# Attention's small products moved to stand in front of p_packed @ w_in, with four PSUM banks as one ring

## The chip, the core and the metric

The kernel runs on one core of a Trainium2 chip. The core has a matrix engine (TensorE; PE is its matmul row and PEld its weight loads in the profile), a vector engine (DVE), a scalar engine (ACT), GpSimd (POOL) and a queue that issues transfers (SP). Matmul results land in PSUM, which holds 8 banks of 512 float32 columns on 128 partitions. The metric is the device time of one execution in microseconds (us), as the median of several runs.

## The reference, cut to what matters

```python
def sm_attn(qq, kk, vv):
    s = scale * np.matmul(qq, kk.transpose(0, 1, 3, 2))
    s = s - np.max(s, axis=-1, keepdims=True)
    a = np.exp(s)
    a = a / (np.sum(a, axis=-1, keepdims=True) + 1e-09)
    return np.matmul(a, vv)
p_packed = sm_attn(p, k, v)               # p: 8 x 8 x 32 x 64; k, v: 8 x 8 x 576 x 64
out = sm_attn(q, p_packed, p_packed)      # q: 8 x 8 x 576 x 64
x = out with the heads side by side       # 4608 x 512
h = x @ w_in                              # w_in: 512 x 2048
g = np.maximum(h, 0.0) + np.log1p(np.exp(-np.abs(h)))
return g @ w_out                          # w_out: 2048 x 512
```

Everything is float32.

## The kernel before, in words

There are 8 batches of 576 tokens. The second attention of a batch is `a2 @ p_packed`, so x @ w_in is computed as `a2 @ (p_packed @ w_in)`. The small product `p_packed @ w_in` comes from `make_m` (line 690, PSUM tiles `psm`), in chunks of 512 of the 2048 hidden columns; two PSUM tiles (one for each group of four heads, which the text calls a half) make one chunk.

A **unit** is one batch `b` and one block `f` of 128 hidden columns (`f` = 0 to 15). For each unit TensorE runs in this order:

- `gemm1` (line 733): 12 matmuls of 288 columns into two PSUM tiles `ph`;
- four tiles `acc` of the second product (line 772): 3 matmuls of 512 columns each, on the hidden block of two units earlier (`LAG` = 2).

In the second unit (`f` = 1) of an even batch the 64 leftover tokens of two batches are added as 16 more tiles `acc_m`. Their inputs `gh_m` and `gl_m` (lines 745 and 746) are split by DVE into eight pieces, each good for two tiles.

`softplus` turns `ph` into `gh` and `gl`: ACT takes Abs of each half of `ph`, then Exp and Ln; DVE's scalar_tensor_tensor (line 761) reads `ph` for the last time. `weights` and `make_m` also split their results on ACT (a cast) and DVE (a subtraction, `ml`, line 706).

The attention of batch `b + 1` runs as a generator, `attention_next`, in the gaps of batch `b`. Each `next` executes it up to the next `yield`, and each step puts its TensorE work between two `acc` tiles. Its TensorE work for one batch is, in the names used below:

- **s1**: scores of p and k, two PSUM tiles `ps`, line 338, 288 columns, four heads side by side in 64*32 pieces of the array; once alone (first half) and once behind pk (second half);
- **pk**: `packed_products` (line 385), weights of the first softmax times v, 96*32 pieces, six rounds of 64 columns;
- **s2**: scores of q and p_packed, made like s1; once behind pk and once alone;
- **psa** (line 377): three transposes a tile, two tiles a half; **psx** (line 420): one transpose a half.

The order on TensorE is the order of the code. On the other engines a scheduler sets it, by the order of the code and its estimates. Up to the twentieth unit (`PINNED` = 20, batch 1's fourth block) the orders of ACT, DVE, POOL and SP are pinned by tables of numbers. A pace sets how often the generator steps: 0.62 of a step for each `acc` tile in batch 1 and 0.56 from batch 2 on. `make_m` of the chunk that unit `u + 2` starts is called at the end of unit `u`.

PSUM: four banks hold `acc`, two (`ps_h`) hold `ph`, and two (`ps_m`) hold everything that `bank()` hands out: `ps`, `psa`, `psx`, `psm`.

Of the kernel before, what the change touches and what calls it, by code (L numbers as in the profile page):

```python
# [9 lines left out]
F32 = mybir.dt.float32  # L10
# [51 lines left out]
def pack_attention_then_softplus_ffn(  # L62
# [11 lines left out]
    B, H, S, D = q.shape  # L74
    J = p.shape[2]
    DM, DFF = w_in.shape
    P = 128
# [3 lines left out]
    C = S // 2  # L81
# [6 lines left out]
    NF = DFF // P  # L88
    NT = S // P
    REST = S - NT * P  # L90
    LAG = 2
    MC = 512
# [10 lines left out]
    ps_h = ctx.enter_context(tc.tile_pool(name="ps_h", bufs=2, space=bass.MemoryType.PSUM))  # L103
    ps_m = ctx.enter_context(tc.tile_pool(name="ps_m", bufs=2, space=bass.MemoryType.PSUM))
# [17 lines left out]
    PW = BG * J  # L122
    pT = const.tile([P, H, PW], F32, name="pT")

    spare = []

    def bank(nm):
        if spare:
            spare.append(spare.pop(0))
            pool, tag = spare[-1]  # L130
            return pool.tile([P, 512], F32, tag=tag, name=nm)
        return ps_m.tile([P, 512], F32, tag="m", name=nm)
# [285 lines left out]
    def packed_transposed(b, g, pp):  # L418
        ps = bank(f"psx_{b}_{g}")
        nc.tensor.transpose(ps[:, :P], pp.rearrange("x i d -> x (i d)"), ident)  # L420
        pt = small.tile([P, P], F32, tag="pt", name=f"pt_{b}_{g}", bufs=2 * G)
        nc.vector.tensor_copy(pt, ps[:, :P])
        return pt
# [158 lines left out]
    def attention_next(b):  # L582


        a1 = [work.tile([P, S], F32, tag="a1", name=f"a1_{b}_{g}") for g in range(G)]
        if b == FIRST:
            for nm in ("k", "v"):
                for g in range(G):
                    load(nm, b, g)
                    yield  # L590
            yield
        kT = [quads("k", b, 0)]
        yield
        yield
        for c in range(2):
            scores1(b, 0, c, kT[0], a1[0])
        yield
        nm = softmax1_max(b, 0, a1[0])
        kT.append(quads("k", b, 1))
        yield  # L600
        load("q", b, 0)
        z = softmax1_exp(b, 0, a1[0], nm)
        yield
        rs = softmax1_sum(b, 0, z)
        yield
        a1T = work.tile([NP, SI, P], F32, tag="a1T", name=f"a1T_{b}_0", bufs=1)
        for c in range(2):
            a1_transposed(b, 0, c, a1[0], a1T)
            yield
        yield  # L610
        ps = [bank(f"ps1_{b}_{c}") for c in range(2)]
        packed_products(b, 0, a1T, ps[0][:, C:C + D])
        s1 = [products1(b, 1, c, kT[1], ps[c]) for c in range(2)]
        for c in range(2):
            nc.scalar.copy(a1[1][:, c * C:(c + 1) * C], s1[c])
        pp = packed_scaled(b, 0, ps[0][:, C:C + D], rs)
        yield
        load("q", b, 1)
        load("k", b + 1, 0)
        nm = softmax1_max(b, 1, a1[1])  # L620
        qT = [quads("q", b, 0)]
        yield
        z = softmax1_exp(b, 1, a1[1], nm)
        res[b]["pt"].append(packed_transposed(b, 0, pp))
        yield
        rs = softmax1_sum(b, 1, z)
        yield
        a1T = work.tile([NP, SI, P], F32, tag="a1T", name=f"a1T_{b}_1", bufs=1)
        for c in range(2):
            a1_transposed(b, 1, c, a1[1], a1T)  # L630
            yield
        load("k", b + 1, 1)
        qT.append(quads("q", b, 1))
        yield
        ps = [bank(f"ps2_{b}_{c}") for c in range(2)]
        packed_products(b, 1, a1T, ps[0][:, C:C + D])
        s2 = [products2(b, 0, c, qT[0], ps[c]) for c in range(2)]
        pp = packed_scaled(b, 1, ps[0][:, C:C + D], rs)
        a2 = work.tile([P, S], F32, tag="a2", name=f"a2_{b}_0", bufs=2)
        for c in range(2):  # L640
            nc.vector.transpose(a2[:, c * C:(c + 1) * C], s2[c])
        yield
        yield
        load("v", b + 1, 0)
        res[b]["pt"].append(packed_transposed(b, 1, pp))
        yield
        softmax2_exp(b, 0, a2)
        yield
        yield
        softmax2_div(b, 0, a2)  # L650
        yield
        a2 = scores2(b, 1, qT[1])
        yield
        softmax2_exp(b, 1, a2)
        yield
        load("v", b + 1, 1)
        yield
        softmax2_div(b, 1, a2)
        yield

# [50 lines left out]
    def gemm1(b, f, res):  # L711

        n = m_cols(b)
        halves = res["m"][f * P // n]
        at_h, at_l = res["at"]
        phs = [
            ps_h.tile([P, 512], F32, tag="h", name=f"ph_{b}_{f}_{c}")[:, :C] for c in range(2)
        ]
        terms = []
        for g in range(G):  # L720
            mh, ml = halves[g * n // MC]
            o = g * n % MC + f * P % n
            ms = slice(o, o + P)
            xy = [(mh, at_h), (mh, at_l), (ml, at_h)]
            if b and f == 0:
                xy.append(xy.pop(1))
            terms += [(x[:, ms], y, g) for x, y in xy]
        turns = [(i, c) for c in range(2) for i in range(3 * G)]
        if b and f == 0:
            turns.sort(key=lambda x: x[0] == 3 * G - 1)  # L730
        for i, c in turns:
            x, y, g = terms[i]
            nc.tensor.matmul(  # L733
                phs[c], x, y[:, g, c * C:(c + 1) * C], start=(i == 0), stop=(i == 3 * G - 1)
            )
        return phs
# [100 lines left out]
    def pin():  # L837

        traced = list(nc.cur_bb.bb.instructions)
        for engine, order in ORDER.items():  # L840
            kinds = [mybir.InstDMACopy] if engine == mybir.EngineType.SP else COMPUTE
            mine = [i for i in traced if i.engine == engine and type(i) in kinds]
            assert sorted(order) == list(range(len(mine))), (engine, len(order), len(mine))
            for n, i in zip(order[1:], order):
                tc.add_manual_dep(
                    mine[n], mine[i].name,
                    mybir.DependencyInfo(mybir.DependencyClass.NoSync, mybir.DependencyReason.DATA),
                )
            ctx.enter_context(tc.issue_after(mine[order[-1]]))

    PACE = [0.64, 0.62] + [0.56] * B
    FRONT = 1000
    CONV = 1.6
    CONV_EARLY = 1.6
# [39 lines left out]
    for u in range(len(units) + LAG):  # L894
        if u == PINNED:
            pin()
        if u < len(units):
            b, f = units[u]
            if f == 0:
                if (b + 1) % BG == 0 and b + 1 < B:  # L900
                    pack_transposed((b + 1) // BG, pt)
                ahead = attention(b + 1) if b + 1 < B else iter(())
                due = 0.0
            chain = softplus(b, f, gemm1(b, f, res[b]), gs)
            next(chain)
            if f == NF - 1:
                if (b + 2) % BG == 0 and b + 2 < B:
                    pt = load_pack((b + 2) // BG, (nc.sync,))
                for _ in ahead:
                    pass  # L910
                if b + 1 < B:
                    weights(b + 1)
        if u >= LAG:
            b2, f2 = units[u - LAG]
            gh, gl = gs.pop((b2, f2))
            if f2 == 0:
                acc = [ps_acc.tile([P, DM], F32, tag="acc", name=f"acc_{b2}_{t}") for t in range(NT)]
        last = u >= LAG and f2 == NF - 1 and b2 % 2 == 1
        if last:
            both = rests(b2)  # L920
            next(both)
        for t in range(NT):
            if u >= LAG:
                gemm2_tile(
                    acc[t], gh, gl, f2, slice(t * P, (t + 1) * P), f2 == 0, f2 == NF - 1
                )
                if f2 == NF - 1:
                    store(acc[t], [(0, b2, t * P, P)], f"{b2}_{t}", t)
            if u < len(units):
                due += PACE[b] if b else STEPS[f * NT + t]  # L930
                while due >= 1:
                    next(ahead, None)
                    due -= 1
                if b == 0:
                    cdue += CONV
                    while cdue >= 1:
                        next(conv, None)
                        cdue -= 1
            next(chain, None)
        if last:  # L940
            next(both)
        if u + 2 < len(units):


            nb, c = units[u + 2][0], units[u + 2][1] * P
            if c % m_cols(nb) == 0:
                make_m(nb, c // m_cols(nb), res[nb])
# [29 lines left out]
```

## Time and profile before

| | |
|---|---|
| median of 3 runs | 748.07 us (747.09 to 749.26) |
| the profiled execution | 747.87 us, its span 746.0 us |
| PE busy | 715.4 us of the span |
| mean granted TensorE clock | 0.991 of full speed |

The span is what the trace covers; 1.9 us of the profiled execution lie outside it. A timeline row gives the start, the length, the engine, the source line, the operation, the tile written and the tiles read, and the count of instructions merged into it. Matmuls are pipelined: a row's length is longer than its distance to the next row, so the distance between starts is the time that TensorE spends on it.

### The profile page before, as it was taken

The page shows a single profiled execution, that of the slowest core. Times are in us where ns is not written, and L with a number is a line of the kernel's source. Part 1 is how long each engine was busy: PE and PEld are TensorE (multiplying, and loading weights), DVE is VectorE, ACT ScalarE, POOL GpSimd, SP SyncE. Part 2 cuts the span into 40 slices and gives each one's busy share as a digit, 9 for nine tenths or more (in the row PEclk, how much of TensorE's full clock was granted, in tenths as well). Part 3 has the DMA queues.
Part 4 walks back from the last instruction along what each step waited for, and adds up shares of the span by engine and source line. Part 5 has one row for each costly group of instructions (what it writes and reads, how often), then busy time and mean ns, then how long its engine had stood idle before and what let it go on. Part 6 is the DMA issues. An engine that isn't in the chain of part 4 may idle for free.

```text
span 746.0 us, 14398 instructions
## 1 busy us (share of the span) xinstructions
PE 715.4 (96%) x5516; PEld 572.2 (77%) x5516; DVE 515.6 (69%) x1068; ACT 421.0 (56%) x1025; POOL 95.9 (13%) x166
## 2 busy tenths in 40 slices
PE   5479999999999999999999999999999999999997
PEld 3357877777878778777788777877788777888885
DVE  3797779857884587667866678566867568565544
ACT  6679877664553545665553555565553455555540
POOL 1425451100000000000000000100000000101110
PEclk9879999999999999999999999999999999999999
DMA  7846662184113431154104431034403110010002
GB/s 285 308 153 232 170 181 38 46 155 81 40 34 70 65 68 30 49 94 82 33 1 100 67 65 33 0 91 72 88 1 81 32 25 1 0 58 1 1 1 71
DMA packets 143044, 55.97 MB, mean 75 GB/s; under 512 B 116352, under 2 KB 130944, under 8 KB 142976
## 3 DMA queue, kind: packets, MB, share of 16 engines
q1 hardware_dynamic: 142704, 55.00, 29.8%
q8 instruction: 43, 0.70, 0.4%
q14 instruction: 25, 0.20, 0.1%
q10 hardware_dynamic: 272, 0.07, 0.0%
HBM read 45.61 MB, written 9.44 MB: 74 GB/s over the span
## 4 chain that ended last, share of the span: by engine, by line
PE 92%; DVE 3%; DMA 2%; ACT 2%; issue 1%; SPq 0%; DVEq 0%; ACTq 0%
PE acc L772 46%; PE ph L733 28%; PE acc_m L772 6%; PE psm L690 5%; PE ps L338 2%; PE ps L385 1%; PE psa L377 1%; DMA v<-in_v 1%; DMA k<-in_k 1%; ACT e L302 1%; PE psp L412 0%; DVE o L793 0%; DVE t L256 0%; PE psT_k L323 0%; DVE a L440 0%
## 5 line engine op out<-in xcount | busy, mean ns | idle before, releaser
L772 PE MATMUL acc<-wo_h,gh 128*128 128x512 f32 x512 | 206.8, 404 | 0.0
L302 ACT ACTIVATE e<-ph 128x288 f32<-128x288 f32 x256 | 102.6, 404 | 177.5 <-PE ph L733 144.6
L772 PE MATMUL acc<-wo_l,gh 128*128 128x512 f32 x512 | 200.9, 392 | 0.0
L772 PE MATMUL acc<-wo_h,gl 128*128 128x512 f32 x512 | 200.6, 392 | 0.0
L302 ACT ACTIVATE e<-e 128x288 f32<-128x288 f32 (+1 forms) x454 | 188.3, 442 | 6.3
L761 DVE SCALAR_TENSOR_TENSOR e<-ph,e 128x288 f32<-128x288 f32 x230 | 102.7, 453 | 126.2 <-ACT e L302 125.4
L733 PE MATMUL ph<-at_h,mh 128*128 128x288 f32 x512 | 156.3, 306 | 9.4 <-ACT at_h L671 9.2
L733 PE MATMUL ph<-at_l,mh 128*128 128x288 f32 x512 | 150.6, 296 | 1.0 <-DVE at_l L672 1.0
L733 PE MATMUL ph<-at_h,ml 128*128 128x288 f32 x512 | 151.4, 296 | 0.0
L733 PEld LDWEIGHTS ph<-at_h,mh 128*128 128x128 f32 x512 | 96.6, 189 | 42.6 <-DVE gl L746 15.1
L765 POOL COPY rest<-e 128x64 f32<-128x64 f32 x128 | 51.0, 401 | 562.3 <-DVE e L761 531.8
L772 PEld LDWEIGHTS acc<-wo_h,gh 128*128 128x128 f32 x512 | 96.1, 188 | 26.2 <-issue 11.6
L772 PEld LDWEIGHTS acc<-wo_h,gl 128*128 128x128 f32 x512 | 96.1, 188 | 21.1
L772 PEld LDWEIGHTS acc<-wo_l,gh 128*128 128x128 f32 x512 | 96.3, 188 | 13.3
L733 PEld LDWEIGHTS ph<-at_l,mh 128*128 128x128 f32 x512 | 96.3, 189 | 4.6 <-DVE at_l L672 1.3
L733 PEld LDWEIGHTS ph<-at_h,ml 128*128 128x128 f32 x512 | 96.6, 189 | 0.2
L746 DVE TENSOR_TENSOR gl<-e,gh 128x512 fp32r<-128x512 f32 x128 | 87.4, 683 | 6.3 <-PE ph L733 0.5
L705 ACT CAST mh<-psm 128x512 fp32r<-128x512 f32 (+1 forms) x72 | 36.1, 541 | 56.4 <-PE psm L690 56.3
L745 DVE CAST gh<-e 128x512 fp32r<-128x512 f32 x128 | 55.6, 435 | 5.8
L706 DVE TENSOR_TENSOR ml<-psm,mh 128x512 fp32r<-128x512 f32 (+1 forms) x72 | 42.6, 623 | 23.9 <-ACT mh L705 23.9
L690 PE MATMUL psm<-w_in_sb,pt 64*32 64x512 f32 (+1 forms) x576 | 37.3, 553 | 0.4 <-ACT T_q L326 0.2
L265 POOL TENSOR_TENSOR r<-t,r 128x512 int32<-128x512 int32 x16 | 22.9, 1433 | 30.6 <-DVE t L256 22.9
(87 smaller groups left out, 663.5 us busy)
## 6 DMA issues: line engine op xcount, KB each, us to landing
v<-in_v SPq DMA_DIRECT2D x16, 576.0 KB, 5.3
x_i<-in_moe_w_in SPq DMA_DIRECT2D x14, 512.0 KB, 4.6
k<-in_k SPq DMA_DIRECT2D x48, 144.0 KB, 3.1
q<-in_q SPq DMA_DIRECT2D x48, 144.0 KB, 3.1
x_o<-in_moe_w_out SPq DMA_DIRECT2D x11, 512.0 KB, 3.7
out<-o SPq DMA_DIRECT2D x18, 256.0 KB, 2.4
rest<-in_moe_w_out SPq DMA_DIRECT2D x5, 512.0 KB, 5.5
out<-o SPq DMA_DIRECT2D x38, 64.0 KB, 1.7
```

The lines of the kernel that those rows point to most:

```text
L265: nc.gpsimd.tensor_tensor(dst if a > 1 else dst.rearrange("x (a n) -> x a n", a=a), *v, op=ALU.add)
L302: return make(*args, **kw)
L338: nc.tensor.matmul(ps[hh * J:(hh + 1) * J, :C], lhs(hh)[c * D:(c + 1) * D], rhs[hh][c * D:(c + 1) * D], start=True, stop=True,)
L690: nc.tensor.matmul(ps[i * J:(i + 1) * J, :n], res["pt"][g][o:o + D, hh * J:(hh + 1) * J], w_in_sb[o:o + D, (g * HG + hh) // 2, c * n:(c + ...
L705: nc.scalar.copy(mh[:, cols], ps[:, :n])
L706: nc.vector.tensor_tensor(ml[:, cols], ps[:, :n], mh[:, cols].bitcast(F32), op=ALU.subtract)
L733: nc.tensor.matmul(phs[c], x, y[:, g, c * C:(c + 1) * C], start=(i == 0), stop=(i == 3 * G - 1))
L745: nc.vector.tensor_copy(hi, x)
L746: nc.vector.tensor_tensor(lo, x, hi.bitcast(F32), op=ALU.subtract)
L761: nc.vector.scalar_tensor_tensor(es[c], hv[c], 0.0, es[c], op0=ALU.max, op1=ALU.add)
L765: nc.gpsimd.tensor_copy(rest[:, rest_at(b, f), r:r + REST], e[:, NT * P:])
L772: nc.tensor.matmul(acc, x[:, cs], y[:, f, :], start=(first and i == 0), stop=(last and i == 2),)
```

## The change

From unit 20 on three things differ.

- **Places.** Attention's steps no longer follow a pace. The list `AT` holds pairs (f, t): behind tile `t` of unit `f` the generator makes one step. The generator has 20 steps a batch now, since some empty yields are gone and the two psa tiles of one half are one step. `make_m` is called behind tile 2 (the third of four) of units 1, 5, 9 and 12, right behind the step at that place, in place of the ends of units 2, 6, 10 and 14. The steps there are s1 (unit 1), pk with s1 (unit 5), pk with s2 (unit 9) and s2 (unit 12; the chunk is the next batch's first).
- **Halves together.** Both psa tiles of a half stand side by side, and psx of the first half stands in front of the psa tiles of the second.
- **Ring.** `ph` and all that `bank()` hands out take their banks in turn from the four banks of `ps_h` and `ps_m`. A tile waits for the last reader of the tile four places earlier.

Batch 1 takes part from its fifth unit on; batch 7 has no attention beside it.

```diff
     def bank(nm):
+        if turn:
+            turn.append(turn.pop(0))
+            pool, tag = turn[-1]
+            return pool.tile([P, 512], F32, tag=tag, name=nm)
...
         for c in range(2):
             a1_transposed(b, 0, c, a1[0], a1T)
-            yield
         yield
...
+        yield
+        rs = softmax1_sum(b, 1, z)
+        yield
         res[b]["pt"].append(packed_transposed(b, 0, pp))
-        yield
-        rs = softmax1_sum(b, 1, z)
-        yield
         a1T = work.tile([NP, SI, P], F32, tag="a1T", name=f"a1T_{b}_1", bufs=1)
         for c in range(2):
             a1_transposed(b, 1, c, a1[1], a1T)
-            yield
+        yield
...
-        phs = [
-            ps_h.tile([P, 512], F32, tag="h", name=f"ph_{b}_{f}_{c}")[:, :C] for c in range(2)
-        ]
+        names = [f"ph_{b}_{f}_{c}" for c in range(2)]
+        if turn:
+            phs = [bank(nm)[:, :C] for nm in names]
+        else:
+            phs = [ps_h.tile([P, 512], F32, tag="h", name=nm)[:, :C] for nm in names]
...
-    PACE = [0.64, 0.62] + [0.56] * B
+    PACE = 0.62
+    TOGETHER = {1: 1, 5: 2, 9: 3, 12: 4}
+    AT = [(0, 1), (0, 3), (1, 2), (1, 3), (2, 1), (2, 3), (3, 2), (5, 2), (5, 3), (6, 1), (6, 3),
...
         if u == PINNED:
             pin()
+            turn += [(ps_h, "h")] * 2 + [(ps_m, "m")] * 2
...
-                due += PACE[b] if b else STEPS[f * NT + t]
+                if u < PINNED:
+                    due += PACE if b else STEPS[f * NT + t]
+                else:
+                    due = (AT_FIRST if b == 1 else AT).count((f, t))
...
+            if PINNED <= u < len(units) and t == 2 and f in TOGETHER:
+                nb, c = divmod(TOGETHER[f], NF * P // MC)
+                if b + nb < B:
+                    make_m(b + nb, c, res[b + nb])
...
-        if u + 2 < len(units):
+        if u + 2 < len(units) and u < PINNED:
```

TensorE in batch 4, before: s2 of batch 5's second half (`ps2_5_1`) and, two tiles later, the chunk `psm_4_3`.

```order
L772 MATMUL acc_4_1_4908<-wo_h_88,gl_4_8_5347 128x512
L338 MATMUL ps2_5_1_0_5434<-q_5_1_5086,pt_5_1_5340 32x288 x4
L338 MATMUL ps2_5_1_1_5440<-q_5_1_5086,pt_5_1_5340 32x288 x4
L772 MATMUL acc_4_2_4909<-wo_h_88,gh_4_8_5346 128x512
L772 MATMUL acc_4_2_4909<-wo_l_89,gh_4_8_5346 128x512
L772 MATMUL acc_4_2_4909<-wo_h_88,gl_4_8_5347 128x512
L772 MATMUL acc_4_3_4910<-wo_h_88,gh_4_8_5346 128x512
L772 MATMUL acc_4_3_4910<-wo_l_89,gh_4_8_5346 128x512
L772 MATMUL acc_4_3_4910<-wo_h_88,gl_4_8_5347 128x512
L690 MATMUL psm_4_3_0_5461<-w_in_sb_87,pt_4_0_4123 32x512 x4
L690 MATMUL psm_4_3_1_5462<-w_in_sb_87,pt_4_1_4328 32x512 x4
```

The same s2 in the changed kernel (unit 12 of batch 4), with batch 5's first chunk `psm_5_0`:

```order
L774 MATMUL acc_4_2_4927<-wo_h_88,gl_4_10_5445 128x512
L342 MATMUL ps2_5_1_0_5536<-q_5_1_5144,pt_5_1_5479 32x288 x4
L342 MATMUL ps2_5_1_1_5542<-q_5_1_5144,pt_5_1_5479 32x288 x4
L690 MATMUL psm_5_0_0_5552<-w_in_sb_87,pt_5_0_5240 32x512 x4
L690 MATMUL psm_5_0_1_5553<-w_in_sb_87,pt_5_1_5479 32x512 x4
L774 MATMUL acc_4_3_4928<-wo_h_88,gh_4_10_5444 128x512
```

Two separate groups of small products between `acc` tiles have become one group.

TensorE in unit 1 of batch 4, before, where s1 of batch 5 stands ahead of the leftover tiles `acc_3_m`:

```order
L772 MATMUL acc_3_1_3896<-wo_h_88,gl_3_15_4694 128x512
L338 MATMUL ps1_5_0_0_4782<-k_5_0_4079,pT_91 32x288 x4
L338 MATMUL ps1_5_0_1_4788<-k_5_0_4079,pT_91 32x288 x4
L772 MATMUL acc_3_2_3897<-wo_h_88,gh_3_15_4693 128x512
L772 MATMUL acc_3_2_3897<-wo_l_89,gh_3_15_4693 128x512
L772 MATMUL acc_3_2_3897<-wo_h_88,gl_3_15_4694 128x512
L772 MATMUL acc_3_3_3898<-wo_h_88,gh_3_15_4693 128x512
L772 MATMUL acc_3_3_3898<-wo_l_89,gh_3_15_4693 128x512
L772 MATMUL acc_3_3_3898<-wo_h_88,gl_3_15_4694 128x512
L772 MATMUL acc_3_m_4817<-wo_h_88,gh_3_m_4767 128x512
```

The same place in the changed kernel:

```order
L774 MATMUL acc_3_2_3915<-wo_h_88,gl_3_15_4694 128x512
L342 MATMUL ps1_5_0_0_4790<-k_5_0_4137,pT_91 32x288 x4
L342 MATMUL ps1_5_0_1_4796<-k_5_0_4137,pT_91 32x288 x4
L690 MATMUL psm_4_1_0_4806<-w_in_sb_87,pt_4_0_4228 32x512 x4
L690 MATMUL psm_4_1_1_4807<-w_in_sb_87,pt_4_1_4467 32x512 x4
L774 MATMUL acc_3_3_3916<-wo_h_88,gh_3_15_4693 128x512
L774 MATMUL acc_3_3_3916<-wo_l_89,gh_3_15_4693 128x512
L774 MATMUL acc_3_3_3916<-wo_h_88,gl_3_15_4694 128x512
L774 MATMUL acc_3_m_4835<-wo_h_88,gh_3_m_4767 128x512
```

s1 stands one tile later, and a chunk of `psm` now stands between it and the leftover tiles.

DVE at that place, before: from the last read of `ph` in unit 1 to the third piece of the leftover input, `gh_3_m` (m1, nm1 and rs belong to batch 5's first softmax).

```order
L761 SCALAR_TENSOR_TENSOR e_4_1_4758<-ph_4_1_1_4745,e_4_1_4758 128x288
L793 COPY o_3_0_4774<-acc_3_1_3896 128x512
L357 TENSOR_REDUCE m1_5_0_4811<-a1_5_0_4729 128x1
L793 COPY o_3_2_4798<-acc_3_2_3897 128x512
L745 CAST gh_4_1_4802<-e_4_1_4758 128x512
L793 COPY o_3_2_4798<-acc_3_3_3898 128x512
L746 TENSOR_TENSOR gl_4_1_4803<-e_4_1_4758,gh_4_1_4802 128x512
L359 TENSOR_SCALAR nm1_5_0_4813<-m1_5_0_4811 128x1
L745 CAST gh_3_m_4767<-rest_90 128x256
```

DVE in the changed kernel, from and to the same rows:

```order
L763 SCALAR_TENSOR_TENSOR e_4_1_4758<-ph_4_1_1_4745,e_4_1_4758 128x288
L795 COPY o_3_0_4774<-acc_3_1_3914 128x512
L795 COPY o_3_2_4786<-acc_3_2_3915 128x512
L361 TENSOR_REDUCE m1_5_0_4829<-a1_5_0_4729 128x1
L363 TENSOR_SCALAR nm1_5_0_4831<-m1_5_0_4829 128x1
L706 TENSOR_TENSOR ml_4_1_0_4817<-psm_4_1_0_4806,mh_4_1_0_4816 128x512
L373 TENSOR_SCALAR rs_5_0_4953<-z1_5_0_4940 128x1
L747 CAST gh_4_1_4802<-e_4_1_4758 128x512
L795 COPY o_3_2_4786<-acc_3_3_3916 128x512
L748 TENSOR_TENSOR gl_4_1_4803<-e_4_1_4758,gh_4_1_4802 128x512
L706 TENSOR_TENSOR ml_4_1_1_4821<-psm_4_1_1_4807,mh_4_1_1_4820 128x512
L747 CAST gh_3_m_4767<-rest_90 128x256
```

The two `ml` of the chunk and `rs`, which reads the row sums of ACT's exponential, have come in front of the third piece. Batch 6 has the same two orders at its unit 1; batch 2 has one more `gh_m` and `gl_m` ahead of them.

## Rows read from the trace of the kernel before

**Rows 1.** The page: busy time of TensorE; its granted clock in 40 slices.

```profile
PE 715.4 (96%) x5516; PEld 572.2 (77%) x5516; DVE 515.6 (69%) x1068; ACT 421.0 (56%) x1025; POOL 95.9 (13%) x166
...
PEclk9879999999999999999999999999999999999999
```

**Rows 2.** Waits of PE from 125 us on: total us, times, longest us.

```profile
PE acc_m L772 <- DVE gh_m L745: 1.1, 1, 1.1
```

**Rows 3.** Timeline of PE, batch 2, unit 1: s1 alone between acc tiles.

```profile
217.34 0.40 PE L772 MATMUL acc<-wo_l,gh 128*128 128x512 f32 x1
217.57 0.40 PE L772 MATMUL acc<-wo_h,gl 128*128 128x512 f32 x1
217.90 0.72 PE L338 MATMUL ps<-k,pT 64*32 64x288 f32 x16
218.54 0.50 PE L772 MATMUL acc<-wo_h,gh 128*128 128x512 f32 x1
218.88 0.40 PE L772 MATMUL acc<-wo_l,gh 128*128 128x512 f32 x1
```

**Rows 4.** Timeline of PE, batch 4, end of unit 2: psm alone.

```profile
410.41 0.39 PE L772 MATMUL acc<-wo_h,gl 128*128 128x512 f32 x1
410.73 1.09 PE L690 MATMUL psm<-w_in_sb,pt 64*32 64x512 f32 x16
411.75 0.40 PE L733 MATMUL ph<-at_h,mh 128*128 128x288 f32 x1
411.98 0.29 PE L733 MATMUL ph<-at_l,mh 128*128 128x288 f32 x1
412.11 0.29 PE L733 MATMUL ph<-at_h,ml 128*128 128x288 f32 x1
```

**Rows 5.** Timeline of PE, batch 4, unit 4: pk and s1 together.

```profile
419.95 0.88 PE L385 MATMUL ps<-v,a1T 96*32 96x64 f32 x48
420.75 0.71 PE L338 MATMUL ps<-k,pT 64*32 64x288 f32 x16
```

**Rows 6.** Timeline of PE, batch 4: three transposes, and one.

```profile
414.13 0.49 PE L377 MATMUL psa<-ident,a 128*96 128x128 f32 x3
414.38 0.47 PE L772 MATMUL acc<-wo_h,gh 128*128 128x512 f32 x1
414.69 0.39 PE L772 MATMUL acc<-wo_l,gh 128*128 128x512 f32 x1
...
425.87 0.27 PE L420 MATMUL psx<-ident,pp 128*128 128x128 f32 x1
425.90 0.48 PE L772 MATMUL acc<-wo_h,gh 128*128 128x512 f32 x1
426.22 0.39 PE L772 MATMUL acc<-wo_l,gh 128*128 128x512 f32 x1
```

**Rows 7.** Timeline of PE, batch 1: psm behind psx.

```profile
164.16 1.55 PE L690 MATMUL psm<-w_in_sb,pt 64*32 64x512 f32 x16
```

**Rows 8.** Timeline of PE, batch 4, unit 1: s1, and leftover piece three.

```profile
393.26 0.71 PE L338 MATMUL ps<-k,pT 64*32 64x288 f32 x16
...
398.13 0.40 PE L772 MATMUL acc_m<-wo_h,gh_m 128*128 128x512 f32 x1
```

**Rows 9.** Timelines of DVE and of ACT at that place.

```profile
393.28 0.81 DVE L761 SCALAR_TENSOR_TENSOR e<-ph,e 128x288 f32<-128x288 f32 x2
...
394.75 0.75 DVE L357 TENSOR_REDUCE m<-a 128x1 f32<-128x576 f32 x1
...
397.56 0.15 DVE L359 TENSOR_SCALAR nm<-m 128x1 f32<-128x1 f32 x1
397.62 0.28 DVE L745 CAST gh_m<-rest 128x256 fp32r<-128x256 f32 x1
...
397.80 0.78 ACT L302 ACTIVATE a<-a,nm 128x576 f32<-128x576 f32 x1 [3.07 <-DVE nm L359]
```

**Rows 10.** The page's groups: DVE's split of psm; busy us, mean ns, idle before.

```profile
L706 DVE TENSOR_TENSOR ml<-psm,mh 128x512 fp32r<-128x512 f32 (+1 forms) x72 | 42.6, 623 | 23.9 <-ACT mh L705 23.9
```

More of the change, by code (lines that the diff above doesn't have):

```diff
@@ L123, in pack_attention_then_softplus_ffn @@
     pT = const.tile([P, H, PW], F32, name="pT")
-    spare = []
+    spare, turn = [], []
     def bank(nm):
+        if turn:
+            turn.append(turn.pop(0))
+            pool, tag = turn[-1]
+            return pool.tile([P, 512], F32, tag=tag, name=nm)
         if spare:
@@ L623, in attention_next @@
         z = softmax1_exp(b, 1, a1[1], nm)
-        res[b]["pt"].append(packed_transposed(b, 0, pp))
         yield
@@ L627, in attention_next @@
         yield
+        res[b]["pt"].append(packed_transposed(b, 0, pp))
         a1T = work.tile([NP, SI, P], F32, tag="a1T", name=f"a1T_{b}_1", bufs=1)
@@ L642, in attention_next @@
         yield
-        yield
         load("v", b + 1, 0)
-        res[b]["pt"].append(packed_transposed(b, 1, pp))
-        yield
         softmax2_exp(b, 0, a2)
         yield
+        res[b]["pt"].append(packed_transposed(b, 1, pp))
         yield
@@ L656, in attention_next @@
         load("v", b + 1, 1)
-        yield
         softmax2_div(b, 1, a2)
@@ L849, in pin @@
             ctx.enter_context(tc.issue_after(mine[order[-1]]))
-    PACE = [0.64, 0.62] + [0.56] * B
+    PACE = 0.62
+    TOGETHER = {1: 1, 5: 2, 9: 3, 12: 4}
+    AT = [(0, 1), (0, 3), (1, 2), (1, 3), (2, 1), (2, 3), (3, 2), (5, 2), (5, 3), (6, 1), (6, 3),
+          (7, 2), (8, 1), (9, 2), (9, 3), (11, 0), (11, 1), (12, 2), (12, 3), (13, 2)]
+    AT_FIRST = [(4, 0), (4, 1), (4, 3)] + AT[7:]
     FRONT = 1000
```

## The prediction, made before the changed kernel ran

> **What bounds the kernel now.** I read the page's busy times and slices first. TensorE is busy for 715.4 of 746.0 us, and from the fourth of 40 slices on its granted clock is at the higher of its two levels, 2.4 GHz [rows 1]. The table of who waits for whom then shows a single wait of TensorE from 125 us on, 1.1 us for the leftover input `gh_m` [rows 2]. So nearly every nanosecond is set by the stream of matmuls itself, and the change can only shorten that stream or put waits into it. DVE at 69% and ACT at 56% [rows 1] matter where TensorE waits for them.
>
> The timeline of TensorE says what the stream loses. Plain `acc` matmuls start 0.23 us apart [rows 3] and plain `ph` matmuls 0.13 us apart [rows 4]. A group of small products in their midst is an island with two shores:
> - s1 alone: it starts 0.33 after the last `acc`, 0.10 more than the pitch; the next `acc` starts 0.64 after it; that one takes 0.34, 0.11 more than the pitch [rows 3]. In all 0.85 us.
> - psm alone: 0.09 before, 1.02 itself, 0.10 behind [rows 4]. In all 1.21 us.
> - Between 288 columns (0.64) and 512 (1.02) lie 224 columns and 0.38 us, 1.70 ns a column. That leaves 0.64 - 288 x 0.0017 = 0.15 us of s1 that don't depend on its columns: the time until its results are out before something else may start.
> - pk takes 0.80 us until s1 starts [rows 5]. Its six rounds of 64 columns need 6 x 64 x 0.0017 = 0.65, and 0.15 remain, once and not six times (which would give 1.55). So rounds of the same tile shape follow each other without the 0.15, and it is paid where the shape changes, here from 96*32 to 64*32.
>
> **The change part by part.**
>
> *Joined islands.* s1, s2 and psm have the same shape, 64*32 [rows 4, 5]. Where one stands in front of psm, the shore behind it (0.11) and the one before psm (0.09) go, and with them the 0.15 if the two follow each other like pk's rounds: 0.35 us a join. If the 0.15 stay, as between pk and s1, it is 0.20. I take 0.35, because the shape doesn't change. The code has four joins a batch in batches 2 to 6 (units 1, 5, 9 and 12) and three in batch 1 (units 5, 9 and 12), 23 in all: 8.1 us at 0.35, 4.6 at 0.20.
>
> The Trainium skill (TensorEngine Tiling (Array Packing), Tiling Modes, Key Properties) says that a change of the tiling mode, not of the tile alone, drains TensorE. By that rule pk to s1 drains, as the row has it, and s1 to psm doesn't, which would give the 8.1; no row of before has s1 directly in front of psm.
>
> *Transposes.* Three transposes cost 0.25 + 0.31 - 0.23 = 0.33 us, one costs 0.03 + 0.32 - 0.23 = 0.12 [rows 6]. So each further one costs 0.105, and hardly 0.02 hang on the island itself. Three joins a batch (psa with psa twice, psx with psa once) save about 0.04 us a batch, 0.2 in all. If the whole 0.08 by which the first `acc` behind is late were saved each time, it would be 3 x 0.08 x 5.5 batches = 1.3; the other end is nothing.
>
> *psx and psm.* In batch 1 one psm stood right behind psx and took 1.55 us [rows 7] where others take 1.09 [rows 4]. With two banks for both, its second half gets psx's bank and must wait for DVE's copy out of it. They stand apart now: 0.5 us saved. (A wait inside a merged row shows as its length, not as idle time.)
>
> *The leftover tiles.* Here something is late next. In unit 1 of batches 2, 4 and 6 the third piece of `gh_m` is wanted in batch 4 at 398.13, and DVE finished it at 397.62 + 0.28 = 397.90 [rows 8, 9]: 0.23 to spare. In the changed kernel the join puts psm ahead of the leftover tiles, so TensorE comes there 1.21 - 0.35 = 0.86 later, at 398.99. DVE's chain starts later too: s1 stands one `acc` tile later (3 x 0.23 = 0.69), so the maximum m1 starts at 394.75 + 0.69 = 395.44. From m1 to `gh_m` it took 2.87 us [rows 9]. Now one copy `o` stands ahead of m1 and leaves this stretch, two `ml` at 0.62 [rows 10] enter, and `rs` of the size of nm1, 0.15 [rows 9]. With the copy at 0.62, being as long as an `ml`, that is 2.87 - 0.62 + 1.24 + 0.15 = 3.64: `gh_m` starts at 399.08 and ends at 399.36, 0.4 late. But `rs` needs the exponential, which needs nm1: nm1 at 396.2, the exponential 0.24 later and 0.78 long [rows 9], to 397.2 and a little more for its sums, where `rs` without a wait would start at 395.44 + 0.75 + 0.15 + 0.62 = 396.96. The 0.3 to 0.5 of waiting there push `gh_4_1`, `o`, `gl_4_1`, `ml_4_1_1` and `gh_m`, which queue behind `rs`: TensorE waits 0.7 to 1.0 us, with the time that a release takes to arrive. I take 1.0. Batch 6 has the same order; batch 2 has another piece in between and as many `ml`, so 1.0 there as well, where 1.1 stand now [rows 2]. The sum is 3 x 1.0 - 1.1 = +1.9 us; the ends are -1.1 (no wait at all) and +2.5 (1.2 each).
>
> *The ring.* psm now takes the banks of the `ph` of its own unit, so it waits until DVE has read them for the last time. At units 1 and 12 only s1 or s2 lies between. In batch 4 DVE's two reads ended at 393.28 + 0.81 = 394.09 [rows 9]; s1 started at 393.26 [rows 8], will start at 393.95, and psm's products follow 0.49 later (288 x 0.0017) at 394.44. That leaves 0.35 us, and psm's first bank comes free 0.4 earlier. At units 5 and 9 pk adds 0.80 to that. The next `gemm1` takes the banks of s1 or s2, with psm (1.02) and an `acc` tile (0.69) in between, while their copies are short. I cost the ring at nothing, covered by these margins. If the 0.35 were missed by 0.1 at each of the 11 places (unit 1 five times, unit 12 six times), it would cost 1.1 us.
>
> *Loads and other engines.* The loads of q, k and v move by a step or two, and SP's queue with them; they are wanted units later. A step moved on ACT or DVE costs nothing while TensorE doesn't wait for it.
>
> **The sum**, made against the profiled execution: 747.87 - 8.1 - 0.2 - 0.5 + 1.9 = 741.0. The median of the runs is 0.2 above that execution: 741.2.
>
> **The rivals.**
> - *The drain stays in the join.* For it: the one seam of small products that the trace has pays it [rows 5]. Against: there the shape changes. 23 x 0.15 = 3.5 less saved: 744.7.
> - *No new wait at the leftover tiles.* For it: 0.4 late without the wait of `rs` is little, and copies may move. Against: DVE's order puts both `ml` in front. It gives back 1.9 + 1.1, 3.0 us: 738.2.
> - *The ring turns into a wait, and the kernel gets slower.* psm holds TensorE at units 1 and 12 until DVE's second read of `ph`, with `acc` and the next `gemm1` queued behind it. That read follows ACT's Abs, Exp and Ln, and ACT sometimes stands still in front of an exponential for nm1, 3.07 us in [rows 9]. If such a wait stood ahead of unit 1's or 12's Abs, psm would wait for it. The gain of 6.9 is gone when the read is late by 0.35 + 6.9 / 11 = 0.98 us at each place; at 1.5 late it costs 11 x 1.15 = 12.7: 753.9. Against it: in the changed order of ACT attention's exponentials stand behind the Ln of units 1, 5, 9 and 12, not ahead of it. The Trainium skill (TensorEngine Tiling (Array Packing), Performance Considerations, PSUM Bottleneck) warns of just this, that tiling speeds up TensorE but not the emptying of PSUM, whose copies may become the bottleneck. The trace agrees that the emptying is the slower side, with 0.35 us to spare; no row shows it short.
> - *The join saves nothing.* psm waits about as long for its bank as the shores cost: the read late by 0.35 + 0.6. About 748.
>
> **How the numbers follow.** Forecast 0.60, drain stays 0.15, no leftover wait 0.12, joins that save nothing 0.07, ring slower 0.06. The range runs from 738.0 (no leftover wait, a little more from the transposes) to 746.0 (drain stays, and the ring missed by 0.1 at each place). A measurement of this kernel can tell about 0.3%, 2.2 us, from no change: faster means below 745.8. Forecast and two rivals lie there, 0.87, less 0.02 for their upper edge: 0.85. Within: 0.09. Slower: 0.06.
>
> **What would show it.** Right: in the timeline psm starts 0.49 after s1 or s2, 0.64 if the drain stays; joined s1 and psm cost 1.71 in place of 2.06. The waits of TensorE show `acc_m` for `gh_m` three times near 1.0, and no psm row is longer than its like by more than 0.1. Wrong: psm rows that are longer, `ph` among TensorE's waits with more than a microsecond in all, or a granted clock below 9 tenths in the slices behind the third.

## The result, and the profile after

The changed kernel takes 739.03 us, median of 4 runs (738.96 to 739.13); the kernel before took 748.0 in 4 runs of the same session (747.09 to 749.26). The ratio is 0.9882, with a 95% interval of 0.987 to 0.9894. The profiled execution took 738.96 us with a span of 737.0, against 747.87 and 746.0 before: 8.9 us less.

The page's first part and the clock row, to be read beside [rows 1]:

```profile
PE 707.6 (96%) x5516; PEld 579.4 (79%) x5516; DVE 514.6 (70%) x1068; ACT 424.0 (58%) x1025; POOL 95.8 (13%) x166
PEclk9779999999999999999999999999999999999999
```

TensorE does the same 5516 matmuls in 7.8 us less of busy time, at the same granted clock: again 9 tenths or more (the upper level, 2.4 GHz) in every slice from the fourth on. DVE and ACT are busy for as long as before within 3 us. So it is the stream of TensorE that became shorter, and it is still what sets the end.

The timeline of TensorE in batch 4, unit 1, shows a join:

```profile
387.53 0.39 PE L774 MATMUL acc<-wo_h,gl 128*128 128x512 f32 x1
387.85 0.72 PE L342 MATMUL ps<-k,pT 64*32 64x288 f32 x16
388.36 1.06 PE L690 MATMUL psm<-w_in_sb,pt 64*32 64x512 f32 x16
389.36 0.50 PE L774 MATMUL acc<-wo_h,gh 128*128 128x512 f32 x1
389.69 0.40 PE L774 MATMUL acc<-wo_l,gh 128*128 128x512 f32 x1
```

psm starts 0.51 after s1, not 0.64 as the `acc` did in [rows 3]: there is no drain in the seam. The first shore (0.32 from the last `acc`, 0.09 over the pitch) and the last one (0.33 instead of 0.23) are each paid once. From 387.53 to 389.69 are 2.16 us, less two pitches of 0.23: 1.70, where s1 and psm alone took 0.85 + 1.21 = 2.06.

The leftover tiles in the same unit, TensorE's timeline:

```profile
392.66 0.39 PE L774 MATMUL acc_m<-wo_h,gl_m 128*128 128x512 f32 x1
393.82 0.50 PE L774 MATMUL acc_m<-wo_h,gh_m 128*128 128x512 f32 x1 [0.78 <-DVE gh_m L747]
394.16 0.40 PE L774 MATMUL acc_m<-wo_l,gh_m 128*128 128x512 f32 x1
```

and what the table of who waits for whom says of them, beside [rows 2] (total us, times, longest):

```profile
PE acc_m L774 <- DVE gh_m L747: 1.5, 2, 0.8
PE acc_m L774 <- DVE rs L373: 0.7, 1, 0.7
```

One wait became three, as forecast. (The second row is batch 2. It names `rs`, which `acc_m` does not read; the third `gh_m` stands just ahead of `rs` in DVE's order and ends at 222.17, and `acc_m` starts at 222.22.) The shown idle time is smaller than what is lost: from 392.66 to 393.82 are 1.16 us, 0.93 over the pitch, and the next start is 0.11 late as well. By starts each of the three costs 1.0 to 1.1 us.

**A ledger from the starts.** Where all time is in one engine's stream, the starts of its matmuls account for it. For every island I took the time from the last large matmul ahead to the second one behind, less two plain pitches, and summed by kind from 156 us on. A wait is a large matmul that starts over 0.05 us later than its pitch after another. In us:

| term | forecast | before | after | measured |
|---|---|---|---|---|
| 23 joins (pk, s and psm of units 1, 5, 9, 12) | -8.1 | 57.1 | 48.8 | -8.3 |
| transposes psa, psx | -0.2 | 8.74 | 8.60 | -0.14 |
| psm behind psx in batch 1 | -0.5 | 1.79 | 1.33 | -0.46 |
| waits at the leftover tiles | +1.9 | 1.48 | 3.25 | +1.8 |
| late starts of `gemm1`: unit 1 of batches 3 and 5 (0.70), unit 12 of batches 4 and 6 (0.19) | none | 0.89 | 0 | -0.89 |
| other large matmuls against their pitch | none | 0.71 | 0.27 | -0.44 |
| sum | -6.9 | | | -8.4 |
| the first 156 us | none | | | -0.57 |

The last two rows together are -9.0, the difference of the spans. The last one is not the change's doing: nearly all of it, 0.56 us, is there when unit 20 begins, where the change sets in. The part up to there has the same order in both, and its waits for the first loads differ from one execution to the next (TensorE waited 2.6 us for the first k before and 1.6 after). In the kernels below this start was 0 to 1.0 us later than in the changed kernel.

### The profile page after: what moved, and what is told of

It reads as the page before. It is cut to its first block, busy times and chain, and to the rows that moved or that the text cites. A ratio compares the mean times of both kernels' runs of the same rounds, so it can differ in the third digit from the quotient of the medians.

```text
span 737.0 us, 14444 instructions
## 1 busy us (share of the span) xinstructions
PE 707.6 (96%) x5516; PEld 579.4 (79%) x5516; DVE 514.6 (70%) x1068; ACT 424.0 (58%) x1025; POOL 95.8 (13%) x166
## 4 chain that ended last, share of the span: by engine, by line
PE 91%; DVE 4%; DMA 2%; ACT 1%; issue 1%; SPq 0%; ACTq 0%
PE acc L774 47%; PE ph L735 28%; PE acc_m L774 5%; PE psm L690 4%; PE ps L342 3%; DMA v<-in_v 1%; PE ps L389 1%; PE psa L381 1%; DMA k<-in_k 1%; DVE o L795 0%; DVE ml L706 0%; PE psp L416 0%; PE psT_k L327 0%; DVE t L260 0%; DVE m L361 0%
## 5 line engine op out<-in xcount | busy, mean ns | idle before, releaser
L735 PE MATMUL ph<-at_h,mh 128*128 128x288 f32 x512 | 153.0, 299 | 8.8 <-ACT at_h L671 8.8
L706 DVE TENSOR_TENSOR ml<-psm,mh 128x512 fp32r<-128x512 f32 (+1 forms) x72 | 44.1, 623 | 4.8 <-ACT mh L705 4.1
L774 PE MATMUL acc_m<-wo_h,gh_m 128*128 128x512 f32 x64 | 25.3, 396 | 2.2 <-DVE gh_m L747 1.5
```

Source lines behind the costliest of these rows:

```text
L706: nc.vector.tensor_tensor(ml[:, cols], ps[:, :n], mh[:, cols].bitcast(F32), op=ALU.subtract)
L735: nc.tensor.matmul(phs[c], x, y[:, g, c * C:(c + 1) * C], start=(i == 0), stop=(i == 3 * G - 1))
L774: nc.tensor.matmul(acc, x[:, cs], y[:, f, :], start=(first and i == 0), stop=(last and i == 2),)
```

## The experiments

In the diffs, "-" is the changed kernel unless the text says otherwise. In all runs the kernel before took 747.9 us (747.92 and 747.94 in the two sessions), and the times and ratios stand against that.

**Is it the seam that saves? One `acc` tile between the step and psm.**

```
-            if PINNED <= u < len(units) and t == 2 and f in TOGETHER:
+            if PINNED <= u < len(units) and t == 3 and f in TOGETHER:
```

> The changed kernel with one acc tile put back between each s1, s2 or pk group and its psm; places, halves and ring stay. Theory (the gain is the two shores and the drain that a join saves, 0.35 us each): all 23 joins come undone, 8.1 us are lost, and since psm then comes 0.35 us later in front of the leftover tiles their three waits shrink by up to 0.35 each: about 746 to 747 us, and in the timeline s1 alone costs 0.85 and psm alone 1.21 again. Rival (the gain came from the ring or from the halves, or from waits that the new places avoid): most of it stays, below 743 us.

Measured: 745.69 us (745.65 to 746.1), ratio 0.9971 (0.9959 to 0.9983), span 743.7, 6.7 us over the changed kernel. The timeline of TensorE in batch 4, unit 1:

```profile
391.99 0.39 PE L774 MATMUL acc<-wo_h,gl 128*128 128x512 f32 x1
392.31 0.71 PE L342 MATMUL ps<-k,pT 64*32 64x288 f32 x16
392.95 0.50 PE L774 MATMUL acc<-wo_h,gh 128*128 128x512 f32 x1
...
393.85 1.09 PE L690 MATMUL psm<-w_in_sb,pt 64*32 64x512 f32 x16
394.87 0.50 PE L774 MATMUL acc_m<-wo_h,gh_m 128*128 128x512 f32 x1
```

With a single tile in between, s1 is again 0.64 long and psm has its own two shores. The islands add up to 70.9 us instead of 62.6, +8.3; the waits are 1.8 less, since `acc_m` now waits in batch 2 alone (1.1 us shown, 1.45 by starts). The time lies 0.3 us under what was expected, because the waits shrank by 1.8 and not by 3 x 0.35. So nearly all of the gain is in the seam, and the leftover waits are the price of it.

**What is the ring worth by itself? The kernel before, with the four banks as one ring.**

```
+            turn += [(ps_h, "h")] * 2 + [(ps_m, "m")] * 2
```

(the other lines are `bank` and `gemm1` as the change has them)

> The kernel before with only the ring of four banks added. Theory: the ring by itself frees psm from psx's bank in batch 1 (0.5 us) and the gemm1 of unit 1 in batches 3 and 5 from the previous unit's second read of ph (0.24 us each): about 747 us. Rival 1: it gives nothing, 748 us, as the prediction had it. Rival 2: it carries several us of the gain, 745 us or less.

Measured: 746.21 us in 10 runs (745.36 to 747.23), ratio 0.9978 (0.9968 to 0.9987), span 744.2, of which 0.5 us less is in the start. This is 0.8 us under the 747 that was expected, and of it the prediction had counted only the 0.5 at psx. Two kinds of place show it. Behind psx, psm is no longer stretched (TensorE, batch 1, beside [rows 7]):

```profile
163.47 0.27 PE L424 MATMUL psx<-ident,pp 128*128 128x128 f32 x1
163.67 1.09 PE L694 MATMUL psm<-w_in_sb,pt 64*32 64x512 f32 x16
```

The other kind the prediction had not seen. Here is the kernel before in batch 3, from unit 0 to unit 1: TensorE, its weight loads (PEld), and DVE.

```profile
308.68 0.39 PE L772 MATMUL acc<-wo_h,gl 128*128 128x512 f32 x1
309.15 0.40 PE L733 MATMUL ph<-at_h,mh 128*128 128x288 f32 x1
309.39 0.29 PE L733 MATMUL ph<-at_l,mh 128*128 128x288 f32 x1
```
```profile
309.15 0.19 PEld L733 LDWEIGHTS ph<-at_h,mh 128*128 128x128 f32 x1 [0.51 <-DVE e L761]
```
```profile
308.64 0.82 DVE L761 SCALAR_TENSOR_TENSOR e<-ph,e 128x288 f32<-128x288 f32 x2 [2.25 <-ACT e L302]
```

`gemm1` of unit 1 starts 0.24 late, and its second matmul 0.11: 0.35 us, here and in batch 5. With two banks for `ph` it takes the banks of the unit before, which DVE is just reading; ACT had made DVE late. The table of PE's waits has no row for `ph` there, because the wait is booked to the weight load; the table of the weight loads (PEld) has it, among five waits of `ph` for `e` with 2.3 us in all. Two more of the five cost time as well: in unit 12 of batches 4 and 6 the first weights wait 0.25 us for the same read, and the second matmul of `gemm1` starts 0.10 late (459.17 to 459.40). With the ring `gemm1` takes two other banks, and none of these four late starts is left. In the changed kernel `gemm1` of batch 3, unit 1, starts a plain pitch behind the last `acc`:

```profile
304.55 0.39 PE L774 MATMUL acc<-wo_h,gl 128*128 128x512 f32 x1
304.78 0.29 PE L735 MATMUL ph<-at_h,mh 128*128 128x288 f32 x1
```

**Does the join need the ring? The changed kernel without it.**

```
-            turn += [(ps_h, "h")] * 2 + [(ps_m, "m")] * 2
```

> The changed kernel with its products joined, but with the four PSUM banks again as two pairs (gemm1's products and the products s, psm each on its own pair), so that psm takes the two banks that s has only just filled. Theory of the prediction (the ring is what lets psm stand directly behind s): psm must wait until the copies of s out of those banks have ended; in the trace of the changed kernel these end 1.0 to 1.3 us behind the last product of s, so each of some 23 joins waits about 1 us: 759 to 767 us, with waits of psm for ACT or DVE that the changed kernel does not show. Rival (the ring is worth only what it gave by itself, 1.7 us, since the copies of s end in time): 740.7 us and islands of 1.71 us as in the changed kernel.

Measured: 774.35 us in one run, span 772.4. That is 35 us more than the changed kernel, beyond the upper end of what was expected. By the starts of TensorE a join with s1 costs 1.0 us more, with pk and s1 1.3, with pk and s2 1.5, with s2 1.75, and psa behind psx 0.6. The place with s2, in batch 3, unit 12: TensorE, then DVE.

```profile
380.99 0.71 PE L342 MATMUL ps<-q,pt 64*32 64x288 f32 x16
382.88 1.43 PE L690 MATMUL psm<-w_in_sb,pt 64*32 64x512 f32 x16 [1.17 <-DVE a L444]
```
```profile
381.21 0.43 DVE L747 CAST gh<-e 128x512 fp32r<-128x512 f32 x1
381.74 0.69 DVE L748 TENSOR_TENSOR gl<-e,gh 128x512 fp32r<-128x512 f32 x1
382.35 0.84 DVE L444 STREAM_TRANSPOSE a<-ps 128x288 f32<-128x288 f32 x2
```

What was expected put the end of the copies at 1.0 to 1.3 us behind s at every join, and the joins with s1 cost that. At s2 the copies stand behind `gh` and `gl` in DVE's queue and end 1.5 us behind s2 (382.35 + 0.84 = 383.19, after 380.99 + 0.71 = 381.70), and that queue is what psm waits for. The rival (the ring is worth only the 1.7 us that it gave alone) is off by 34 us: **the join without the ring is 26 us slower than the kernel before.** The two parts are one change.

**How wide is the ring's margin? The joins one tile earlier.**

```
-    AT = [(0, 1), (0, 3), (1, 2), (1, 3), (2, 1), (2, 3), (3, 2), (5, 2), (5, 3), (6, 1), (6, 3),
-          (7, 2), (8, 1), (9, 2), (9, 3), (11, 0), (11, 1), (12, 2), (12, 3), (13, 2)]
+    AT = [(0, 1), (0, 3), (1, 1), (1, 3), (2, 1), (2, 3), (3, 2), (5, 1), (5, 3), (6, 1), (6, 3),
+          (7, 2), (8, 1), (9, 1), (9, 3), (11, 0), (11, 1), (12, 1), (12, 3), (13, 2)]
...
-            if PINNED <= u < len(units) and t == 2 and f in TOGETHER:
+            if PINNED <= u < len(units) and t == 1 and f in TOGETHER:
```

> The changed kernel with all joins one acc tile earlier (behind the second tile of units 1, 5, 9 and 12). Theory (psm takes the banks of its own unit's ph and has 0.35 us to spare at units 1 and 12): 0.69 us earlier it must wait 0.34 us or a little more at 11 places, 3.7 us, seen as longer psm rows there and not at units 5 and 9; the leftover waits shrink by up to 0.69 each, 2.1 us: about 740.5 us. Rival (the banks are free much sooner, or the wait isn't on the banks): no longer psm rows, about 737 us.

Measured: 742.68 us (742.56 to 742.87), ratio 0.9929 (0.9914 to 0.9944), span 740.7. An `acc` tile is 0.69 us, so with 0.35 to spare each join at units 1 and 12 should be 0.34 late. TensorE in batch 4, unit 1, and the weight loads:

```profile
389.19 0.71 PE L342 MATMUL ps<-k,pT 64*32 64x288 f32 x16
389.71 1.43 PE L690 MATMUL psm<-w_in_sb,pt 64*32 64x512 f32 x16
391.06 0.50 PE L774 MATMUL acc<-wo_h,gh 128*128 128x512 f32 x1
```
```profile
390.07 0.15 PEld L690 LDWEIGHTS psm<-w_in_sb,pt 64*32 64x32 f32 x8 [0.21 <-DVE e L763]
```

psm is 1.43 long instead of 1.06, and its second half's weights wait until DVE has read `ph` for the last time (389.20 + 0.81 = 390.01). Ten of the 11 islands are 0.34 to 0.38 longer, one 0.65; those at units 5 and 9, with pk in between, are unchanged at 2.51 to 2.52. The one with 0.65 is unit 1 of batch 2. There a copy `o` stands between DVE's two reads of `ph`, and the second one ends late. In the changed kernel, DVE and TensorE:

```profile
216.35 0.44 DVE L763 SCALAR_TENSOR_TENSOR e<-ph,e 128x288 f32<-128x288 f32 x1
```
```profile
216.88 1.06 PE L690 MATMUL psm<-w_in_sb,pt 64*32 64x512 f32 x16
```

The read ends at 216.79, 0.09 us ahead of psm. **In the changed kernel the margin is 0.35 to 0.40 us at ten of the 11 places, as worked out for batch 4, and 0.09 at this one.** In all the islands are 4.3 us longer where 3.7 was expected, only 1.0 us comes back at the leftover tiles, half of what was hoped for, and the start is 0.4 later: so the time is 2.2 us over what was expected.

**Is the drain paid by shape? psm in front of attention's products instead of behind.**

```
             if PINNED <= u < len(units) and t == 2 and f in TOGETHER:
                 nb, c = divmod(TOGETHER[f], NF * P // MC)
                 if b + nb < B:
                     make_m(b + nb, c, res[b + nb])
```

(these lines, moved from behind the attention step to ahead of it)

> The changed kernel with psm in front of attention's products instead of behind them, in the same place of the unit: psm, then s; and psm, then pk, then s. Theory (a join saves .35 us because nothing of another tile shape runs between two groups of the 64*32 shape, where the array drains): the islands of s and psm stay at 1.71 us, those with pk, which has another shape and now stands between two groups of 64*32, go from 2.52 to 2.67 us, 11 or 12 places. Rival (any small products that stand next to each other save the same, whatever their shape): 2.52 us there as well. In time, psm now takes the two banks that the next unit's gemm1 needs first, .7 us of acc products later, and these are free only when ACT and DVE have copied psm: 740.8 us if the copies end in time, up to 1 us more at each join, 763 us, if they do not. The islands decide between the theories, not the total.

Measured: 744.24 us in one run, span 742.4. The islands decide. TensorE in batch 5, unit 5, first here and then in the changed kernel:

```profile
503.54 0.39 PE L774 MATMUL acc<-wo_h,gl 128*128 128x512 f32 x1
503.86 1.09 PE L690 MATMUL psm<-w_in_sb,pt 64*32 64x512 f32 x16
504.88 0.88 PE L389 MATMUL ps<-v,a1T 96*32 96x64 f32 x48
505.69 0.71 PE L342 MATMUL ps<-k,pT 64*32 64x288 f32 x16
506.33 0.50 PE L774 MATMUL acc<-wo_h,gh 128*128 128x512 f32 x1
```
```profile
499.43 0.39 PE L774 MATMUL acc<-wo_h,gl 128*128 128x512 f32 x1
499.75 0.88 PE L389 MATMUL ps<-v,a1T 96*32 96x64 f32 x48
500.55 0.71 PE L342 MATMUL ps<-k,pT 64*32 64x288 f32 x16
501.06 1.06 PE L690 MATMUL psm<-w_in_sb,pt 64*32 64x512 f32 x16
502.06 0.50 PE L774 MATMUL acc<-wo_h,gh 128*128 128x512 f32 x1
```

From the last `acc` ahead to the first one behind: 2.79 us here and 2.63 there. pk's 96*32 now stands between two groups of 64*32 and there is one more change of shape; all 12 such islands cost 2.67 to 2.70 instead of 2.51, and the 11 without pk stay at 1.70. The rival, that any neighbours save alike, falls. Of the 5.4 us over the changed kernel's span these islands are 1.9 and a later start 0.3. The rest are waits, 3.1 more in all: psm has the two banks that the next `gemm1` wants. TensorE's weight loads, and DVE, ahead of unit 13 of batch 4:

```profile
461.67 0.19 PEld L735 LDWEIGHTS ph<-at_h,mh 128*128 128x128 f32 x1 [0.46 <-DVE ml L706]
```
```profile
460.93 0.69 DVE L706 TENSOR_TENSOR ml<-psm,mh 128x512 fp32r<-128x512 f32 x1 [0.31 <-ACT mh L705]
```

**What do the transposes save? Each half's two turns apart again.** (The `yield` behind each of the two loops over `a1_transposed` in `attention_next` stands inside the loop again; 12 turns more in the whole kernel.)

```
-    AT = [(0, 1), (0, 3), (1, 2), (1, 3), (2, 1), (2, 3), (3, 2), (5, 2), (5, 3), (6, 1), (6, 3),
-          (7, 2), (8, 1), (9, 2), (9, 3), (11, 0), (11, 1), (12, 2), (12, 3), (13, 2)]
-    AT_FIRST = [(4, 0), (4, 1), (4, 3)] + AT[7:]
+    AT = [(0, 1), (0, 3), (1, 2), (1, 3), (2, 1), (2, 3), (3, 2), (4, 0), (5, 2), (5, 3), (6, 1), (6, 3),
+          (7, 2), (8, 0), (8, 1), (9, 2), (9, 3), (11, 0), (11, 1), (12, 2), (12, 3), (13, 2)]
+    AT_FIRST = [(4, 0), (4, 1), (4, 3), (5, 0)] + AT[8:]
```

> The changed kernel with the transposes psa of a half's two tiles in separate turns, an acc tile between them, 12 places more; products joined as before. Theory of the prediction (transposes run over all columns of the array, so standing apart costs only a few hundredths each, .2 us for all): at most 739.3 us. Rival (every place where small products stand apart costs .1 us or more of its own): 740.3 us or more.

Measured: 739.56 us (739.06 to 739.96), ratio 0.9889 (0.9874 to 0.9904), span 737.5. By the starts of the units it loses 0.42 us, 0.035 a turn, of which the islands show 0.1 in all and the matmuls behind them the rest. That is a little over the theory's bound and well under the rival's. The reason given with the theory is loose: the psa tiles are 128*96 [rows 6], not all columns of the array; the price of a turn is what was measured.

**Can the leftover waits be avoided? Batches 2, 4 and 6 with the first join in unit 2.**

```
+    AT_EVEN = AT[:2] + [(2, 2), (2, 3), (3, 1), (3, 3), (4, 2)] + AT[7:]
...
-                    due = (AT_FIRST if b == 1 else AT).count((f, t))
+                    due = (AT_FIRST if b == 1 else AT if b % 2 else AT_EVEN).count((f, t))
...
+            at = TOGETHER if b % 2 else {2 if x == 1 else x: y for x, y in TOGETHER.items()}
```

> The changed kernel, but in batches 2, 4 and 6 the first join (s1 with psm) stands in unit 2 instead of unit 1, behind the leftover tiles; the steps that follow it move up to one unit later. Theory (psm's two ml on DVE and rs in front of the third piece of gh_m make TensorE wait about 1.05 us in each of the three batches): these waits go, about 736 us. Rival (the waits only move: to psa, whose exponential now has a unit less, or to another piece): 738 to 740 us.

Measured: 738.27 us (738.0 to 738.87), ratio 0.9871 (0.9856 to 0.9886), span 736.7. The rival came. In batches 4 and 6 the wait falls from 1.1 to 0.3 us. In batch 2 it grows and changes its place (TensorE, unit 1):

```profile
219.85 0.39 PE L774 MATMUL acc_m<-wo_l,gh_m 128*128 128x512 f32 x1
221.19 0.50 PE L774 MATMUL acc_m<-wo_h,gl_m 128*128 128x512 f32 x1 [0.95 <-DVE gl_m L748]
```

DVE does two transposes of k there, 0.77 us each, that it does elsewhere in batches 4 and 6, and `gl_m` of the second piece stood behind the four copies of `acc`.

**The same, with the second piece written ahead of those copies.** (In `rests` the `split` of the piece becomes a function of its own, and the first two are called ahead of the first `yield`.)

```
-            split(gh[:, cs], gl[:, cs], rest[:, o:o + n, :].rearrange("x f j -> x (f j)"))
+            if i != n:
+                piece(i)
             if i == 0:
+                piece(n)
                 yield
```

> The kernel with the first join of batches 2, 4 and 6 in unit 2, and besides it DVE's second piece of the leftover tiles written in front of the four copies of acc, not behind them. Theory (in batch 2, where two transposes of k take DVE's time, the product acc_m of piece 2 waits 1.1 us only because gl_m of that piece is queued behind the copies): this wait goes down to the .2 to .3 us that batches 4 and 6 show, the rest is unchanged: 737.2 us, span about 735.6. Rival (DVE is full there and the wait moves to piece 3 or to the next unit's gemm1): 738.3 us as without this edit.

Measured: 737.53 us (736.71 to 737.64), ratio 0.9859 (0.9842 to 0.9875), span 735.6. The time is 0.3 above the expected one and the mechanism a mixture. The wait for `gl_m` (1.2 us by starts) has shrunk to 0.3 us, and another one, at the first `acc_m`, has grown from 0.3 to 0.6 us (TensorE, batch 2, unit 1):

```profile
217.08 0.39 PE L774 MATMUL acc<-wo_h,gl 128*128 128x512 f32 x1
217.83 0.50 PE L774 MATMUL acc_m<-wo_h,gh_m 128*128 128x512 f32 x1 [0.36 <-DVE o L795]
```

The bank of `acc_m` is one that the first of those copies must have emptied, and `gl_m` now stands ahead of it. All leftover waits together are 1.5 us by starts, against 3.25 in the changed kernel. This kernel's runs all lie below those of the changed kernel (738.96 to 739.13): it is the best version found here, by 1.5 us.

## Why the prediction was right, step by step

The forecast was 741.2 and the time 739.0; the sign, the mechanism and the order of the terms held, and the sum was 2.2 us short.

- **The joins, 0.35 each.** 8.3 us measured for 8.1, 0.36 a join. That no drain stands in the seam is in the timeline (0.51 between starts), and the two experiments on it leave no other cause: a tile between brings all 8.3 us of islands back, and a change of shape between brings 0.16 back. The rule of the Trainium skill on which the prediction leant (TensorEngine Tiling (Array Packing), Tiling Modes, Key Properties) says that changing the mode, not merely the tile, drains the engine; the trace agrees for these tiles (64*32, 96*32 and 128*128), with 0.15 to 0.16 us a change; the 128*96 of psa beside 128*128 shows no such price. The rival with the drain in the join (744.7) and the one with joins that save nothing (748) fall with it.
- **The transposes and psx with psm.** 0.14 and 0.46 measured for 0.2 and 0.5. That standing alone costs a transpose next to nothing held for the islands; with the matmuls behind them, the experiment with the halves apart shows 0.4 us for all, twice the forecast.
- **The leftover tiles.** Three waits of 1.0 to 1.1 us for three of 1.0. DVE and ACT went the way that was worked out; their rows in batch 4 beside [rows 9]:

```profile
387.20 0.81 DVE L763 SCALAR_TENSOR_TENSOR e<-ph,e 128x288 f32<-128x288 f32 x2
...
389.34 0.75 DVE L361 TENSOR_REDUCE m<-a 128x1 f32<-128x576 f32 x1
390.13 0.15 DVE L363 TENSOR_SCALAR nm<-m 128x1 f32<-128x1 f32 x1
...
391.28 0.15 DVE L373 TENSOR_SCALAR rs<-z 128x1 f32<-128x1 f32 x1 [0.40 <-ACT a L306]
...
393.48 0.28 DVE L747 CAST gh_m<-rest 128x256 fp32r<-128x256 f32 x1
```
```profile
390.38 0.78 ACT L306 ACTIVATE a<-a,nm 128x576 f32<-128x576 f32 x1 [0.31 <-DVE nm L363]
```

  This trace is 6.10 us ahead of the times of the prediction (s1 at 387.85 for 393.95). With that taken off, m1 was forecast for 389.34 and nm1 for 390.10; they came at 389.34 and 390.13. `rs` waits 0.40 us for ACT's exponential, forecast 0.3 to 0.5, and `gh_m` starts at 393.48, forecast 393.3 to 393.5. The small error is on the other side: before, the wait in batch 2 cost 1.48 us by starts and not the 1.1 that the table showed; after, the three cost 3.25 and not 3.0. The step cost 1.8 instead of 1.9. The rival without a new wait (738.2) gives nearly the time that was measured, but by a path that the trace excludes: the waits came.
- **The ring at nothing, covered by 0.35 us.** The cover held: DVE's last read of `ph` ends at 387.20 + 0.81 = 388.01, psm starts at 388.36, and a join one tile earlier pays just the difference. But the margin was worked out in batch 4 alone and taken for all 11 places; at unit 1 of batch 2 it was 0.09 us, and that this was enough is luck. The rival in which the ring turns into a wait (753.9) falls, and the experiment without the ring shows what it would have been like. **Here the step also failed in its size:** nothing was taken for what the ring gives `gemm1`. It takes away 0.89 us of late starts in batches 3 to 6 that stood in the trace of before. I had read the table of PE's waits, which has no row for them, and not the starts.
- **What no step had.** 0.44 us are large matmuls elsewhere that keep their pitch a little better. The number of islands, 39 fewer, doesn't give it: with the halves apart, 11 islands more in the counted part bring 0.33 us of it back, with a tile between, 23 more bring back 0.14. So it seems to go mostly with the transposes; it was not tried by itself, and why it is so stays open. 0.57 us lie in the first 156 us and are not the change's.

So of the 2.2 us between the forecast and the measured median, 0.9 are the late starts that the ring took away, 0.4 the pitch, 0.6 the start, 0.1 the leftover waits and 0.1 the joins with the transposes and psx; 0.1 is the median, which stands nearer to the profiled execution than the one before did.

## What to carry to other kernels

Where one engine's stream sets the end, cost an edit by the starts in its timeline: what a group of instructions adds over the plain pitch, and how much of that hangs on its edges; then groups of the same tile shape belong next to each other, with no other shape in between. A join needs its output space free earlier than before: work out who empties those banks, what stands ahead in that engine's queue, and how many tenths of a microsecond remain, at every place where the join stands and not at one of them. And look at what is consumed right behind the group: what the stream gains by coming earlier is partly given back where the next input is not earlier.

## What the runs showed of the hardware that I had not expected

- A wait can be absent from the table of PE's waits and yet cost time. The 0.35 us at 308.68 in the kernel before stand only with the weight load (0.51 us of its idle time) and between the starts of the matmuls. Inside a merged row, as psm at 1.43 us instead of 1.06, a wait shows as length.
- Behind a wait the next start is late as well: 393.82 to 394.16 is 0.34 us where the pitch is 0.23. A wait shown as 0.78 us cost 1.04 (0.93 and 0.11), and with a later start in the same unit 1.10.
- In a group of products into two banks, the weights of the second bank's products waited for that bank by themselves (390.07, 0.06 us after DVE's read ended) while the first bank's products were running; the wait is not for both banks at the start of the group.
